# One TensorE loop for all eight V units of a decode attention kernel, and one PSUM bank for all rows of wo

## The chip, the cores and the metric

The kernel runs on one core of a Trainium2 chip. The metric is the device time of one execution in microseconds. The profile is one execution taken by the hardware profiler; its times count from the span's start. The engines are TensorE (PE; PEld is its loading of weights), VectorE (DVE), ScalarE (ACT), GpSimd (POOL) and SyncE (SP), which issues the loads. Each engine works its own list of instructions in order, and 16 DMA engines serve the transfers.

## The reference, cut to what matters

```
q = (x @ wq) as 32 heads of 128          # x: 2 x 1 x 512
scores = q k^T / sqrt(128)               # k_cache, v_cache: 2 x 32 x 4096 x 128, bf16
o = softmax(scores) @ v
a = o @ wo                               # wo: 4096 x 512
b = relu(x @ w1) @ w2                    # w1: 512 x 1376, w2: 1376 x 512
g = sigmoid(sum(x * gate_w))
return g * a + (1 - g) * b
```

K and V are 67 MB each; nearly all bytes are theirs.

## The kernel before, in words

The program is written as one list of instructions for each engine (`P.add` and its short forms `pe`, `dve`, `act`, `pool`, `sp`). The order of the calls from line 732 on is the order in each engine's list. `P.resolve` numbers the instructions that signal, and `P.emit` writes the lists with their waits. A `_Loop` in PE's list becomes a hardware loop (line 99), whose `head_slot` asks that its first instruction stand at the start of a block of instruction memory.

**Loads.** K and V are each eight units of 8 MB. SP issues all loads in one queue, in the order of `pieces` (line 247), into five SBUF regions of 4 MB (`kv`: A, Ah, B, Bh, C). A load waits until the region's last reader is done (`holder`, lines 253 to 264). V's units 0 to 6 are one load each, into A with Ah or B with Bh in turn; unit 7 is two loads, into B and Bh. Behind them stand w2x (the first 96 rows of w2), wo in two parts cut at row 24 of 32 (lines 340 to 342) and w2 in three parts into Ah (lines 343 to 345), which wait for V's unit 6 to be read.

**K.** DVE transposes each quarter of 1 MB (`k_turn`, 64 of them, line 477), PE multiplies it with q in a loop of eight turns run eight times (`k_scores`, lines 504 and 483). Line 483 is the helper `mm_held`, a matmul that uses the weights already loaded; groups of many places carry its number.

**Softmax and V's weights.** After `softmax` DVE spreads the transposed exponentials of a unit over eight columns (`v_spread`), so that they serve as matmul weights. Unit 0 has its weights in two halves (line 549).

**V.** Unit 0 (`v_unit`, line 588) uses weights of 32 columns: four matmuls at a time stand in the four column quarters of the array. Units 1 to 6 are a loop of two units run three times (`v_loop`, lines 617 and 483): weights of 64 columns, each used by two matmuls, into two PSUM banks. In the loop, counting semaphores stand for the usual waits: `sem_pt` (weights ready), `sem_v` (load landed) and `sem_rd` (the unit before is done). The two halves of unit 7 are `v_unit(7)` and `v_unit(8)`, 32 matmuls each. `v_extract` (lines 629, 641) takes a unit's result out of PSUM on DVE: for a loop unit three masked products, two of them on 32 partitions, then a sum.

**The end.** `o_gather(b)` adds up the units of one batch on PE (line 657), `o_scale(b)` scales the sum on DVE (line 663), `o_turn` turns it into `oW` (lines 669, 672). `project` (line 684) multiplies the four extra w2 rows (numbers -4 to -1) and wo's rows 0 to 23 into one PSUM bank in four column quarters; `pr_copy` (line 689) copies the bank to SBUF. `last_rows` multiplies wo's rows 24 to 31, then a row with `sel2` that adds up the copied bank, then w2's ten rows, all as small matmuls into the bank of the result (`fin_row`, line 697; `held_row`, lines 704 to 712). `store` copies the result out. `idle(n)` are n matmuls whose result nobody reads; they keep PE busy.

Of the kernel before, what the change touches and what calls it, by code (L numbers as in the profile page):

```python
# [17 lines left out]
WO_CUT = 24  # L18
WIDE = 5

# [37 lines left out]
class _Prog:  # L58
# [13 lines left out]
    def resolve(self):  # L72
        for e in self.ENGINES:
            n = 0
            for op in self.ops[e]:
                if isinstance(op, _Loop):
                    for m in range(op.n):
                        for step in op.ops:
                            if step.markers:
                                n += 1  # L80
                                step.markers[m].engine = e
                                step.markers[m].idx = n
                elif op.marker is not None:
                    assert op.marker.engine is None, "marker signalled twice"
                    n += 1
                    op.marker.engine = e
                    op.marker.idx = n

    def emit(self, engine, eng):
# [7 lines left out]
        for op in self.ops[engine]:  # L97
            if isinstance(op, _Loop):
                with self.nc.Fori(0, op.n, engines=(eng.engine,), head_slot={eng.engine: 0}):
                    for step in op.ops:  # L100
                        for sem, val in step.waits:
                            eng.wait_ge(sem, val)
                        ins = step.fn(eng)
                        if step.markers:
                            ins.then_inc(self.sems[engine], 1)
                continue
# [16 lines left out]
def bass_gated_mix__gqa_block_cached__dense_activation_relu__decode_kernel(  # L123
# [80 lines left out]
    V_BS = {0: 4, 7: 4, 8: 2}  # L204
    V_PAIRS = ((2, 3), (5, 6))
    V_LOOP = range(1, 7)
# [7 lines left out]
    O_C0 = MISC + 128  # L214
# [30 lines left out]
    v_pieces = [(u, both, "AB"[u % 2]) for u in range(7)] + [(7, lo, "B"), (7, hi, "Bh")]  # L245
# [9 lines left out]
    for kind, n, u, halves, region in pieces:  # L255
        parts = [region, region + "h"] if len(halves) == 2 else [region]
        predecessor[kind, n] = [m for r in parts for m in holder[r]]
        if kind == "v" and n in V_LOOP:
            landed[kind, n] = (sem_v[(n + 1) % 2], None)
# [227 lines left out]
    def k_scores():  # L487
# [27 lines left out]
        for bank in range(4):  # L515
            pe(lambda e, bank=bank: e.matmul(psf(0, 128, bank * BANK, 512), lhsT=ident16[:, :], rhs=zeros, start=False, stop=True),  # L516
               signal="pe_sc_end" if bank == 3 else None)

    def softmax():
# [10 lines left out]
        for g in range(2):  # L530
# [7 lines left out]
            v_spread_first(g)  # L538
        dve(lambda v: v.tensor_reduce(out=lrow[:], in_=lsum[:], axis=AX.X, op=ALU.add), waits=["act_exp3"], signal="dve_lrow")

    v_at = [0, 2, 4, 2, 4, 2, 4, 0, 1]

    def v_weights(n):
        nh = len(v_pieces[n][1])
        return ptm[:, 1024 * v_at[n]:1024 * (v_at[n] + nh)].rearrange("p (n h c) -> p n h c", h=8, c=4)

    def v_spread_first(g):
        rows, shape = slice(32 * g, 32 * g + 32), [128, 32, 8, 4]
        dve(lambda v: v.tensor_tensor(out=v_weights(0)[:, rows], in0=ET_sb[:, rows, 0:4].unsqueeze(2).to_broadcast(shape),  # L549
                                      in1=mask8[:].unsqueeze(1).unsqueeze(3).to_broadcast(shape), op=ALU.mult),  # L550
            waits=[f"dve_et{g}", "c_mask8"], signal=f"pt0{g}")

    def v_spread(n):
        u, halves, region = v_pieces[n]
        w0 = 4 * u + 2 * halves[0]
        waits = ["dve_et1", "c_mask8"] + ([f"v_read_{n - 2}"] if 3 <= n < 7 else ["v_read_0"] if n >= 7 else [])

        def spread(out, src, nc_, **kw):
            shape = [128, src.shape[1], 8, nc_]
            def fn(v):  # L560
                ins = v.tensor_tensor(out=out, in0=src.unsqueeze(2).to_broadcast(shape),  # L561
                                      in1=mask8[:].unsqueeze(1).unsqueeze(3).to_broadcast(shape), op=ALU.mult)
                return ins.then_inc(sem_pt[(n + 1) % 2], 1) if n in V_LOOP else ins
            dve(fn, waits=waits, **kw)

        if len(halves) == 2:
            spread(v_weights(n), ET_sb[:, :, w0:w0 + 4], 4)
        else:
            for r2 in range(2):
                spread(v_weights(n)[:, :, :, r2:4:2], ET_sb[:, 32 * r2:32 * r2 + 32, w0:w0 + 2], 2, signal=(f"pt{n}" if r2 else None))  # L570
# [4 lines left out]

    def v_unit(n):
        rows = v_moving(n)
        nn = rows.shape[2]
        for j in range(nn):
            t = j % 4  # L580
            waits = []
            if n == 0 and j % 32 == 0:
                waits = [f"pt0{j // 32}"]
            elif j == 0:
                waits = [f"pt{n}", "dve_m0" if n == 7 else "dve_m5"]

            def fn(e, j=j, t=t):
                ins = e.matmul(psf(32 * t, 32 * t + 32, V_BS[n] * BANK, 512), lhsT=v_weights(n)[:, j],  # L588
                               rhs=rows[:, :, j, :], start=(j < 4), stop=(j >= nn - 4), tile_position=(0, 32 * t))
                return ins.then_inc(sem_rd[1], 1) if n == 0 and j == nn - 2 else ins  # L590
            pe(fn, waits=waits, dwaits=([landed["v", n]] if j == 0 else []), signal=(f"v_read_{n}" if j == nn - 1 else None))

    def idle(n):
        out, lhsT, rhs = psf(0, 32, IDLE_C0, 512), ident16[:, 0:32], qbuf[:, :, :, :, 0:32]
        for j in range(n):
            if j:
                pe(lambda e: mm_held(e, out, lhsT, rhs, True, True, (128, 32), (0, 0)))
            else:
                pe(lambda e: e.matmul(out, lhsT=lhsT, rhs=rhs, start=True, stop=True, tile_position=(0, 0)), waits=["dve_m5"])

    def v_loop():
        loop = _Loop(len(V_LOOP) // 2)
        P.ops["pe"].append(loop)
        for x in range(2):
            n0 = V_LOOP[x]
            rows = v_moving(n0)
            for k in range(64):
                t, side = (k // 2) % 2, k % 2

                def fn(e, k=k, t=t, side=side, rows=rows, x=x, n0=n0):  # L610
                    out = psf(64 * t, 64 * t + 64, V_PAIRS[x][side] * BANK, 512)
                    lhsT = v_weights(n0)[:, k - side:k - side + 2].rearrange("p n h c -> p (n h c)")
                    start, stop = k < 4, k >= 60
                    if side:
                        ins = mm_held(e, out, lhsT, rows[:, :, k, :], start, stop, (128, 64), (0, 64 * t))
                    else:
                        ins = e.matmul(out, lhsT=lhsT, rhs=rows[:, :, k, :], start=start, stop=stop, tile_position=(0, 64 * t))  # L617
                    take = {0: (sem_pt[x], -1), 1: (sem_v[x], -16), 2: (sem_rd[1 - x], -1), 62: (sem_rd[x], 1)}.get(k)
                    return ins.then_inc(*take) if take else ins
                waits = [(sem_rd[1 - x], 1), (sem_pt[x], 1), (sem_v[x], 16)] if k == 0 else []  # L620
                marks = [marker(f"v_read_{V_LOOP[2 * m + x]}") for m in range(loop.n)] if k == 63 else None
                loop.ops.append(_Step(fn, waits, marks))

    def v_extract(n):
# [8 lines left out]
        waits = [f"v_read_{n}", "dve_maskc"] + ([f"dve_x{n - 1}"] if n else [])  # L633
        if n in V_LOOP:
            first, second = V_PAIRS[(n + 1) % 2]
            masked(first, 0, 128, waits, f"dve_ma{n}")
            masked(second, 32, 64, [f"dve_ma{n}"], f"dve_mb{n}")
            masked(second, 96, 128, [f"dve_mb{n}"], f"dve_m{n}")
        else:
            masked(V_BS[n], 0, 128, waits, f"dve_m{n}")  # L640
# [12 lines left out]
    def o_gather(b, part):  # L653
        mine = range(n_first) if b == 0 else range(n_first, len(v_pieces))
        for n in part:
            w0 = 24 - 8 * (v_pieces[n][0] - 4 * b)
            pe(lambda e, n=n, w0=w0: e.matmul(psf(0, 32, O_C0, 128), lhsT=selx[:, w0:w0 + 32], rhs=X2[:, b, n - mine[0], :],
                                              start=(n == mine[0]), stop=(n == mine[-1])),
               waits=[f"dve_x{n}"] + (["dve_rinv", "dve_selx"] + (["dve_O0"] if b else []) if n == mine[0] else []),
               signal=(f"pe_O{b}" if n == mine[-1] else None))  # L660

    def o_scale(b):
        dve(lambda v, b=b: v.tensor_scalar(out=O_sb[:, b, :], in0=psf(0, 32, O_C0, 128), scalar1=rinv[:, b:b + 1],
# [14 lines left out]
    def project(rows):  # L678
        for r in rows:
            t = r % 4  # L680
            lhsT, rhs = (hT[:, 14 + r, BOTH], w2x[:, t, :]) if r < 0 else (oW[:, r, BOTH], wreg[:, r * 512:(r + 1) * 512])
            dw = {-4: [(sem["w2x"], 32)], 0: [(sem["wo0"], 16)]}.get(r, [])
            waits = {-4: ["dve_h2", "dve_pr0"], 0: ["dve_oW"]}.get(r, [])
            pe(lambda e, t=t, r=r, lhsT=lhsT, rhs=rhs: e.matmul(psf(32 * t, 32 * t + 2, PR_C0, 512), lhsT=lhsT, rhs=rhs,
                                                               start=(r < 0), stop=(r >= WO_CUT - 4), tile_position=(0, 32 * t)),
               dwaits=dw, waits=waits, signal=("pe_pr" if r == WO_CUT - 1 else None))

# [28 lines left out]
    def last_rows():  # L716
        for r in range(WO_CUT, 32):
            fin_row(r == WO_CUT, False, oW[:, r, :], wreg[:, r * 512:(r + 1) * 512], [(sem["wo1"], 16)] if r == WO_CUT else [], [])
        fin_row(False, False, sel2[:, :], pr_sb, [], ["dve_pr", "dve_sel2"])
# [23 lines left out]
    v_spread(2)  # L743
    v_unit(0)
    o_denominators()
    v_loop()
    v_extract(0)
    for n in (last - 1, last):
        v_spread(n)
    for n in V_LOOP:  # L750
        v_extract(n)
        if n + 2 in V_LOOP:
            v_spread(n + 2)
    o_gather(0, range(n_first))
    o_scale(0)
    pr_clear()
    v_unit(last - 1)
    idle(6)
    v_extract(last - 1)
    o_gather(1, range(n_first, last - 1))  # L760
    idle(5)
    o_gather(1, (last - 1,))
    idle(13)
    v_unit(last)
    v_extract(last)
    project(range(-4, 0))
    idle(7)
# [4 lines left out]
    project(range(WO_CUT))  # L772
# [36 lines left out]
```

## Time and profile before

| | us |
|---|---|
| median of 3 runs (lowest, highest) | 343.67 (343.65, 343.81) |
| the profiled execution | 343.51 |
| its span, first to last instruction | 342.2 |
| busy: PE / DVE / ACT / POOL | 228.1 / 197.4 / 9.9 / 14.2 |
| mean granted TensorE clock | 0.865 |

A page of the profile has the busy time of each engine, the DMA queues, the chain of work that ended last, and the costliest groups by line. In the chain, each piece of work is followed back to what released it. In the timeline, "[1.25 <-DMA x]" means that the engine had sat idle for 1.25 us until the load of x landed. Ends of matmuls are modelled: the next may stream some 0.18 us before the end shown.

### The profile page before, as it was taken

The page shows a single profiled execution, that of the slowest core. Times are in us where ns is not written, and L with a number is a line of the kernel's source. Part 1 is how long each engine was busy: PE and PEld are TensorE (multiplying, and loading weights), DVE is VectorE, ACT ScalarE, POOL GpSimd, SP SyncE. Part 2 cuts the span into 40 slices and gives each one's busy share as a digit, 9 for nine tenths or more (in the row PEclk, how much of TensorE's full clock was granted, in tenths as well). Part 3 has the DMA queues.
Part 4 walks back from the last instruction along what each step waited for, and adds up shares of the span by engine and source line. Part 5 has one row for each costly group of instructions (what it writes and reads, how often), then busy time and mean ns, then how long its engine had stood idle before and what let it go on. Part 6 is the DMA issues. An engine that isn't in the chain of part 4 may idle for free.

```text
span 342.2 us, 2434 instructions
## 1 busy us (share of the span) xinstructions
PE 228.1 (67%) x1279; PEld 54.0 (16%) x770; DVE 197.4 (58%) x139; ACT 9.9 (3%) x29; POOL 14.2 (4%) x41
## 2 busy tenths in 40 slices
PE   0467329799969799689799463809172552909976
PEld 0111001111111111111111120202020110202313
DVE  1239059899889899698999496140606032020621
ACT  1051000000000000000000110000000000000000
POOL 6000000000000000000000200000000000000000
PEclk9999959989989899999999967856769585767999
DMA  8998989899999999898989999999989999989995
GB/s 349 429 490 370 483 375 483 371 486 414 444 467 391 426 433 483 383 475 375 483 383 475 398 467 423 429 467 391 483 383 475 391 467 391 467 387 433 426 421 241
DMA packets 3793, 145.50 MB, mean 425 GB/s; under 512 B 429, under 2 KB 564, under 8 KB 844
## 3 DMA queue, kind: packets, MB, share of 16 engines
q1 hardware_dynamic: 3782, 145.43, 98.6%
q8 instruction: 4, 0.07, 0.1%
q14 instruction: 1, 0.01, 0.0%
q10 hardware_dynamic: 6, 0.00, 0.0%
HBM read 145.43 MB, written 0.00 MB: 425 GB/s over the span
## 4 chain that ended last, share of the span: by engine, by line
DMA 63%; DVE 19%; PE 15%; issue 2%; ACT 0%; SPq 0%; DVEq 0%
DMA kv<-in_A_k_cache_dram 32%; DMA kv<-in_A_v_cache_dram 24%; DVE kt L477 17%; DMA kv<-in_B_w_dram 7%; PE PS L483 6%; PE PS L617 4%; PE PS L504 2%; PE PS L588 1%; DVE mpad L520 1%; ACT kt L532 0%; DVE kt L536 0%; DVE kt L549 0%; PE PS L697 0%; PE PS L516 0%; SPq L332 0%
## 5 line engine op out<-in xcount | busy, mean ns | idle before, releaser
L477 DVE STREAM_TRANSPOSE kt<-kv 128x2048 f32<-128x2048 f32 x64 | 141.2, 2274 | 25.7 <-DMA kv<-in_A_k_cache_dram 25.7
L504 PE MATMUL PS<-kt,qbuf 128*128 128x512 bf16 x256 | 106.2, 415 | 31.3 <-issue 23.0
L483 PE MATMUL PS<-kt,qbuf 128*128 128x512 bf16 x256 | 106.1, 415 | 0.0
L617 PE MATMUL PS<-kv,kt 128*64 128x512 bf16 x192 | 47.4, 471 | 55.2 <-DMA kv<-in_A_v_cache_dram 55.2
L629 DVE TENSOR_TENSOR kt<-PS,maskc 32x512 f32<-32x512 f32 (+1 forms) x21 | 14.5, 689 | 88.3 <-PE PS L483 81.3
L504 PEld LDWEIGHTS PS<-kt,qbuf 128*128 128x128 bf16 x256 | 25.7, 100 | 140.7 <-issue 140.7
L483 PE MATMUL PS<-kv,kt 128*64 128x512 bf16 x192 | 46.8, 465 | 0.0
L617 PEld LDWEIGHTS PS<-kv,kt 128*64 128x64 bf16 x192 | 15.2, 135 | 96.1 <-issue 96.1
L561 DVE TENSOR_TENSOR kt<-kt,mask 128x2048 bf16<-128x2048 bf16 (+1 forms) x10 | 16.2, 1656 | 0.0
L588 PE MATMUL PS<-kv,kt 128*32 128x512 bf16 x128 | 8.9, 432 | 8.6 <-DVE kt L549 7.3
L401 POOL TENSOR_TENSOR qbuf<-qs,mask 128x64 bf16<-128x64 bf16 x16 | 6.5, 406 | 160.7 <-PE PS L483 141.1
L641 DVE TENSOR_REDUCE kt<-kt 128x128 f32<-128x512 f32 x9 | 9.2, 1025 | 0.3
L483 PE MATMUL PS<-qbuf,ident 128*32 128x512 bf16 x37 | 9.0, 379 | 0.0
L406 PE MATMUL PS<-kv,xTw 128*32 128x320 bf16 (+1 forms) x32 | 5.3, 691 | 5.2 <-DMA kv<-in_A_wq_dram 3.2
L532 ACT ACTIVATE kt<-PS,negm 128x512 bf16<-128x512 f32 x4 | 2.7, 686 | 168.9 <-DVE negm L528 168.9
L588 PEld LDWEIGHTS PS<-kv,kt 128*32 128x32 bf16 x128 | 3.9, 107 | 15.6 <-DVE kt L549 7.8
L430 DVE CAST qrow<-PS 128x256 bf16<-128x256 f32 x2 | 2.6, 1524 | 5.7 <-PE PS L483 5.7
L729 ACT ACTIVATE out_sb<-PS 4x128 bf16<-4x128 f32 x1 | 0.3, 267 | 142.3 <-PE PS L712 142.3
L353 PE MATMUL PS<-ident,x_sb 3*128 3x3 bf16 x4 | 0.3, 166 | 6.2 <-DMA x_sb<-in_gate_w_dram 6.2
L520 DVE TENSOR_REDUCE mpad<-PS 128x2 f32<-128x2048 f32 x1 | 2.3, 2292 | 3.1 <-PE PS L516 3.1
L356 DVE COPY xT<-PS 128x12 bf16<-128x12 bf16 x1 | 0.2, 171 | 6.5 <-PE PS L353 6.5
L483 PE MATMUL PS<-kv,xTw 128*32 128x512 bf16 (+1 forms) x24 | 3.7, 511 | 0.0
(88 smaller groups left out, 53.6 us busy)
## 6 DMA issues: line engine op xcount, KB each, us to landing
kv<-in_A_k_cache_dram SPq DMA_DIRECT2D x4, 4096.0 KB, 29.4
kv<-in_A_v_cache_dram SPq DMA_DIRECT2D x2, 4096.0 KB, 23.5
kv<-in_A_wq_dram SPq DMA_DIRECT2D x1, 4096.0 KB, 14.8
kv<-in_A_wo_dram SPq DMA_DIRECT2D x1, 3072.0 KB, 33.4
kv<-in_B_w_dram SPq DMA_DIRECT2D x1, 1376.0 KB, 5.6
kv<-in_A_wo_dram SPq DMA_DIRECT2D x1, 1024.0 KB, 35.4
kv<-in_B_w_dram SPq DMA_DIRECT2D x1, 896.0 KB, 22.3
kv<-in_B_w_dram SPq DMA_DIRECT2D x1, 256.0 KB, 22.6
```

The lines of the kernel that those rows point to most:

```text
L401: pool(lambda g: g.tensor_tensor(out=out, in0=src, in1=mask, op=ALU.mult).then_inc(sem_q[k % 2], 1), waits=waits)
L406: return e.matmul(out, lhsT=xTw[:, t, :], rhs=rhs, start=(t == 0), stop=(t == 3), tile_position=(0, 32 * c))
L477: dve(lambda v: v.transpose(out=dst, in_=pairs[:, h, 64 * a:64 * a + 64, :]).then_inc(sem_kt[i % SPAN], 1), waits=([f"pe_sc_{i - NKT}"] if ...
L483: return e.add_instruction(mybir.InstMatmult(start_tensor_calc=start, stop_tensor_calc=stop, tile_size=size, tile_position=at, ldweights=F ...
L504: ins = e.matmul(out, lhsT=lhsT, rhs=rhs, start=False, stop=False)
L520: dve(lambda v: v.tensor_reduce(out=mpad[:, 0:2], in_=psf(0, 128, 0, 4 * BANK).rearrange("p (par n) -> p par n", par=2), axis=AX.X, op=ALU ...
L532: act(lambda a, g=g, par=par: a.activation(out=E_sb[:, 32 * g:32 * g + 32, 16 * par:16 * par + 16], in_=psf(0, 128, (2 * par + g) * BANK, ...
L561: ins = v.tensor_tensor(out=out, in0=src.unsqueeze(2).to_broadcast(shape), in1=mask8[:].unsqueeze(1).unsqueeze(3).to_broadcast(shape), op= ...
L588: ins = e.matmul(psf(32 * t, 32 * t + 32, V_BS[n] * BANK, 512), lhsT=v_weights(n)[:, j], rhs=rows[:, :, j, :], start=(j < 4), stop=(j >= n ...
L617: ins = e.matmul(out, lhsT=lhsT, rhs=rows[:, :, k, :], start=start, stop=stop, tile_position=(0, 64 * t))
L629: dve(lambda e: e.tensor_tensor(out=parts[p0:p1], in0=psf(p0, p1, bank * BANK, 512).rearrange("p (c d) -> p c d", c=4), in1=maskc[p0:p1].u ...
L641: dve(lambda e: e.tensor_reduce(out=X2[:, b, k, :], in_=parts.rearrange("p c d -> p d c"), axis=AX.X, op=ALU.add), waits=[f"dve_m{n}"], si ...
```

## The change

- V's unit 7 becomes one load (`v_pieces`), and all eight units are one PE loop of two units run four times, 64 matmuls of 32-column weights each, into bank 4 or 5. `v_unit`, the 64-column pairs and the second banks go. `sem_rd`, which tells the loop that the unit before is done, gets its first count from the first closing matmul of the scores.
- Behind the even unit of each round stand 55 idle matmuls: one, and an inner loop of nine run six times.
- Both loops are written without `head_slot`.
- Unit 0 waits for both halves of its weights, and stands behind the two denominator matmuls. `v_spread(2)` moves behind `v_extract(0)`.
- `v_extract` is one masked product and the sum for every unit.
- All earlier gathers on PE, and `o_scale(0)` on DVE, stand behind the loop and ahead of unit 7's extract; the second batch's gather has a bank of its own. `pr_clear` moves up. The idle matmuls there: `idle(6)`, `idle(5)` and `idle(13)` go, `idle(7)` becomes `idle(4)`.
- `project` takes all 32 rows of wo, waiting for wo's second part at row 24; `pr_copy` comes after all of them, and `last_rows` begins with sel2's row.

The diff, cut to its core:

```diff
-                with self.nc.Fori(0, op.n, engines=(eng.engine,), head_slot={eng.engine: 0}):
+        with self.nc.Fori(0, loop.n, engines=(eng.engine,)):
...
-    v_pieces = [(u, both, "AB"[u % 2]) for u in range(7)] + [(7, lo, "B"), (7, hi, "Bh")]
+    v_pieces = [(u, both, "AB"[u % 2]) for u in range(8)]
...
+            def close(e, bank=bank):
+                ins = e.matmul(psf(0, 128, bank * BANK, 512), lhsT=ident16[:, :], rhs=zeros, start=False, stop=True)
+                return ins if bank else ins.then_inc(sem_rd[1], 1)
...
     def v_loop():
-        loop = _Loop(len(V_LOOP) // 2)
+        loop = _Loop(len(v_pieces) // 2)
         P.ops["pe"].append(loop)
         for x in range(2):
-            n0 = V_LOOP[x]
-            rows = v_moving(n0)
-            for k in range(64):
-                t, side = (k // 2) % 2, k % 2
+            rows = v_moving(x)
+            for j in range(64):
+                t = j % 4
...
+                    ins = e.matmul(psf(32 * t, 32 * t + 32, V_BANK[x] * BANK, 512), lhsT=v_weights(x)[:, j], rhs=rows[:, :, j, :],
+                                   start=(j < 4), stop=(j >= 60), tile_position=(0, 32 * t))
...
+            if x == 0:
+                out, lhsT, rhs = psf(0, 32, IDLE_C0, 512), ident16[:, 0:32], qbuf[:, :, :, :, 0:32]
+                loop.ops.append(_Step(lambda e: e.matmul(out, lhsT=lhsT, rhs=rhs, start=True, stop=True, tile_position=(0, 0)), [], None))
+                inner = _Loop(IDLE_ROUNDS)
+                for j in range(IDLE_EACH):
+                    inner.ops.append(_Step(lambda e: mm_held(e, out, lhsT, rhs, True, True, (128, 32), (0, 0)), [], None))
+                loop.ops.append(inner)
...
-        if n in V_LOOP:
-            first, second = V_PAIRS[(n + 1) % 2]
-            masked(first, 0, 128, waits, f"dve_ma{n}")
-            masked(second, 32, 64, [f"dve_ma{n}"], f"dve_mb{n}")
-            masked(second, 96, 128, [f"dve_mb{n}"], f"dve_m{n}")
-        else:
-            masked(V_BS[n], 0, 128, waits, f"dve_m{n}")
+        masked(V_BANK[n % 2], 0, 128, [f"v_read_{n}", "dve_maskc"] + ([f"dve_x{n - 1}"] if n else []), f"dve_m{n}")
...
-                                                               start=(r < 0), stop=(r >= WO_CUT - 4), tile_position=(0, 32 * t)),
-               dwaits=dw, waits=waits, signal=("pe_pr" if r == WO_CUT - 1 else None))
+                                                               start=(r < 0), stop=(r >= WO_ALL - 4), tile_position=(0, 32 * t)),
+               dwaits=dw, waits=waits, signal=("pe_pr" if r == WO_ALL - 1 else None))
...
-        for r in range(WO_CUT, 32):
-            fin_row(r == WO_CUT, False, oW[:, r, :], wreg[:, r * 512:(r + 1) * 512], [(sem["wo1"], 16)] if r == WO_CUT else [], [])
-        fin_row(False, False, sel2[:, :], pr_sb, [], ["dve_pr", "dve_sel2"])
+        fin_row(True, False, sel2[:, :], pr_sb, [], ["dve_pr", "dve_sel2"])
...
     v_spread(1)
-    v_spread(2)
-    v_unit(0)
     o_denominators()
     v_loop()
-    v_extract(0)
-    for n in (last - 1, last):
-        v_spread(n)
-    for n in V_LOOP:
+    pr_clear()
+    for n in range(last):
         v_extract(n)
-        if n + 2 in V_LOOP:
+        if n + 2 <= last:
             v_spread(n + 2)
     o_gather(0, range(n_first))
+    o_gather(1, range(n_first, last))
     o_scale(0)
-    pr_clear()
-    v_unit(last - 1)
-    idle(6)
-    v_extract(last - 1)
-    o_gather(1, range(n_first, last - 1))
-    idle(5)
-    o_gather(1, (last - 1,))
-    idle(13)
-    v_unit(last)
     v_extract(last)
     project(range(-4, 0))
-    idle(7)
+    idle(4)
     o_gather(1, (last,))
     o_scale(1)
     o_turn()
     idle(8)
-    project(range(WO_CUT))
+    project(range(WO_ALL))
     idle(4)
     pr_copy()
     last_rows()
```

## The prediction

> **What bounds the kernel now.** I read the page's DMA queues first, then the chain of waits, then the timeline of the last 40 us, because the first two say that only the end can move.
>
> ```profile
> span 342.2 us, 2434 instructions
> q1 hardware_dynamic: 3782, 145.43, 98.6%
> q8 instruction: 4, 0.07, 0.1%
> ```
>
> The queue q1 carries all loads, and its packets fill 98.6% of 16 engines' span. The missing 1.4% is 4.8 us, about what lies before the first packet and after the last landing. So nothing that TensorE (PE) or VectorE (DVE) does in the middle can pay unless it starves the queue; the change moves the same 145 MB. The time is the landing of the last loads plus what is done after them. The chain of waits, in order of time, ends so (start, us, what):
>
> ```profile
> 278.88 29.07 DMA kv<-in_A_v_cache_dram
> 317.01 22.33 DMA kv<-in_B_w_dram
> 339.39 1.17 PE PS L697 x36
> 340.71 0.28 DVE out_sb L728
> ```
>
> It goes from V's unit 6 to w2's rows, landing at 339.38; PE multiplies them (L697, held row 340.39), DVE and ACT copy out (340.71), the store ends the span at 342.25. V's own tail is not in the chain: the timeline shows it beside the landing of wo (start, us, engine, line; in brackets the wait before it).
>
> ```profile
> 327.42 1.91 PE L588 MATMUL PS<-kv,kt 128*32 128x512 bf16 x32 [1.25 <-DMA kv<-in_A_v_cache_dram]
> 329.38 0.69 DVE L629 TENSOR_TENSOR kt<-PS,maskc 128x512 f32<-128x512 f32 x1 [6.47 <-PE PS L588]
> 330.11 1.04 DVE L641 TENSOR_REDUCE kt<-kt 128x128 f32<-128x512 f32 x1
> 331.19 0.41 PE L657 MATMUL PS<-kt,selx 128*32 128x128 f32 x2 [0.15 <-DVE kt L641]
> 332.31 0.39 PE L599 MATMUL PS<-qbuf,ident 128*32 128x512 bf16 x1
> 334.83 1.47 PE L684 MATMUL PS<-kv,oW 128*2 128x512 bf16 x24 [0.62 <-DMA kv<-in_A_wo_dram]
> 336.35 0.69 DVE L689 COPY kt<-PS 128x512 f32<-128x512 f32 x1 [3.59 <-PE PS L684]
> 337.21 0.87 PEld L697 LDWEIGHTS PS<-kv,oW 128*4 128x4 bf16 x32 [1.20 <-DMA kv<-in_A_wo_dram]
> 338.10 0.60 PE L697 MATMUL PS<-kt,sel 128*4 128x128 f32 x8
> 339.38 0.98 PEld L697 LDWEIGHTS PS<-kv,hT 128*4 128x4 bf16 x36 [0.97 <-DMA kv<-in_B_w_dram]
> ```
>
> Everything here waits for a load: project for wo's first part (334.83), the last eight rows for its second (337.21), w2's rows for theirs (339.38). The slack is small: the turn's copy into oW is over at 332.76, the idle matmuls at about 334.0, and sel2's row 0.7 us before w2 lands.
>
> **The middle, at nothing.** V's units 1 to 6 change from pairs of 64 columns (8.9 us a unit, 308.08 to 317.01, at a clock of 0.55 to 312.1 and then 1.00) to fours of 32 columns. Line 588 shows that shape: four matmuls share 0.43 us at half clock (200.03 to 200.46) and 0.2155 us at full, so a unit is 3.5 to 6.9 us. It frees its region sooner, but the next load then only queues longer. DVE loses two small masked products a unit and waits for loads anyway. The 55 idle matmuls behind each even unit take 55 x 0.2155 = 11.9 us on PE and delay unit 1 (211.30 in the trace) to about 220; its region is then free near 223.6, before V2 lands (230.53). All of that lies under q1.
>
> **The last unit, on the path.** Unit 7 was two loads, the first half multiplied from 317.70; now it is one, complete when the second half was, at about 327.4.
> - Start: unit 6 starts at 308.1 at half clock. 16 groups at 0.2155, made longer by half of the 2.7 to 6.5 us until the clock rises (2.8 us in unit 0, 6.1 in unit 2), end at 313 to 314.8; the idle matmuls end at 325 to 326.6. PE is free when V lands: no delay.
> - Matmuls: 64 are 16 x 0.2155 + 0.18 = 3.63 us against 1.91. Unit 7 ends at 331.05, +1.72.
> - A new wait. Both gathers of earlier units now stand behind the loop in PE's order, and DVE's order has o_scale(0), which waits for the first, ahead of unit 7's extract. The gather is 8 passes, 1.06 us (316.89 in the trace, 0.08 before the modelled end of the unit); the scale takes 0.40. So the extract starts at 331.05 - 0.08 + 1.06 + 0.04 + 0.40 + 0.03 = 332.50 instead of 0.05 after the unit's end: +1.40 more. PE's own queue behind the unit (gathers 0.81 and 0.64, four rows of w2x 0.22, idle(4) 0.86) ends before the extract does, so it hides.
> - Extract to gather: 0.73 + 1.04 + 0.04, at 334.31. From gather to the idle matmuls the trace has 1.12 us (331.19 to 332.31): 335.43. idle(8) is 8 x 0.2155 = 1.72, and project queues behind it: 337.15, where it waited for wo until 334.83. The slack of 2.0 us is gone and 2.3 us are lost.
>
> **wo through one bank.** Project now takes 32 rows: 8 x 0.2155 + 0.18 = 1.90 us, over at 339.05; row 24 is reached at 338.44, after its load (337.21). The 32 small matmuls of rows 24 to 31 (0.84 us) go. The copy of the bank, formerly early (336.35) and hidden under wo's second part, now comes after all rows: 0.05 + 0.69, at 339.79. Sel2's row starts at 339.84; 8 passes start 43 ns apart, so w2's rows start near 340.2 against 339.39. All of w2 has landed by then: 1.00 us to the held row as before, at 341.2 against 340.39. **Sum: +0.8 us.** Had the last unit not been late, the moved copy would end at 337.21 + 0.61 + 0.74 = 338.56 and sel2's row at 339.0, still hidden: it costs because the unit is late.
>
> The profiled execution took 343.51 (span 342.2 and 1.3 around it): 343.51 + 0.8 = 344.3. The median shown is 343.67, 0.16 above it, so I forecast 344.5. Unsure are the loop's exit (0.1), sel2's row (0.15) and when the one load lands (0.2 either way): 344.1 to 344.9 for this case.
>
> **Prices without a row.** The first unit now starts only after both halves of its weights and the denominators (202.6 instead of 199.62) and ends at 208.1 to 209.7, where it ended at 204.66. V2's load is issued then. From issue to landing the smallest transfer (the store, 341.02 to 342.2) takes 1.2 us, so data come at 209.4 to 211.0; unit 1 finds V1 landed at 211.30. Nothing is lost, by 0.2 to 1.8 us; lost would be at most about 1 us.
> The loops lose the alignment of their first instruction, and V's body grows from 192 to 256 matmuls and weight loads, with idle ones besides. The page shows four instruction packets: 0.1% of 16 x 342.2 us is 5.5 us, some 1.4 us each on one DMA engine. A load lands when its slowest engine is done, and in the windows 338 to 339 and 339 to 340 the DMA share falls to 0.61 and 0.24: some engines are about a microsecond behind the others. So one fetch more or fewer on the slowest engine moves landings by 1.4 us either way. I take nothing, the nearest case, since fetches have hit few engines so far.
>
> **Rivals.**
> - *Fewer fetches, faster or the same (0.10).* The PE program gets shorter. If the engine that sets V's last landing loses one fetch less, unit 7 starts 1.4 us sooner and all terms follow: 344.5 - 1.4 = 343.1. It decides from 0.8 us on. For it: the falling DMA share. Against: one early fetch is enough to make a straggler.
> - *The tail stays hidden, the same (0.12).* If the gather before o_scale(0) and sel2's row overlap better than the modelled ends say, 0.8 us vanish: 343.7.
> - *More fetches, slower (0.13).* [...] Over 16 fetches hit engines twice: landings 1.4 us later, 345.9. If the small idle loop itself fetched in each of its six rounds, unit 7 would start many microseconds late; I see no reason for that.
> [...]
> - *The clock falls, slower (0.10).* If PE has dropped to half clock when unit 7 starts, 3.4 us of it run at half speed: +1.7, 346.2. The gap between the idle matmuls and V's landing is 0.8 to 2.4 us. In the trace a stretch of 3.4 us with 1.42 us of busy PE (257.5 to 260.9) kept full clock, and one with 0.82 (278.0 to 281.4) lost it. Only the longest gap comes near.
> [...]
> - *V2 issued late, slower (0.05):* 345.5.
>
> **How the numbers follow.** The forecast has 0.50. A measurement of this kernel can tell 0.2%, 0.7 us, from no change; the line lies at 344.36, inside the forecast's own range, so a quarter of it (0.12) counts as same. Same: 0.12 + 0.12 + 0.04 of the first rival = 0.28. Faster: 0.06. Slower: 0.38 + 0.13 + 0.10 + 0.05 = 0.66. The range runs from 343.4 to 346.2, the hidden tail to the fallen clock, and leaves out some 0.15.
>
> **What would show it.** Unit 7: 64 matmuls in 3.6 us from about 327.4; o_scale(0) between its end and its extract; project not waiting for wo; w2's rows waiting for sel2's row and no longer for DMA; their start near 340.2. A chain that still ends with w2's landing refutes the sum; a landing of V other than 327.4 and a number on q8 other than 4 point to the fetches; unit 7 over 5 us long, to the clock.

## The result, and the profile after

| | us |
|---|---|
| before, median of 6 runs (lowest, highest) | 343.76 (343.65, 343.81) |
| after, median of 6 runs (lowest, highest) | 346.25 (345.21, 347.16) |
| ratio, 95% interval | 1.0074 (1.0056 to 1.0092) |
| the profiled execution of after, and its span | 347.16, 345.9 |

The kernel became slower, by 2.5 us at the median where 0.8 was forecast, and its runs now spread over 2 us where they spread over 0.2. The profiled execution is the slowest of the six, so its distances are the upper end of what the change does. It is 3.65 us longer than the profiled execution of before (347.16 against 343.51).

The page of after, span and DMA queues (packets, MB, share of 16 engines' span):

```profile
span 345.9 us, 2803 instructions
...
q1 hardware_dynamic: 3638, 145.43, 97.6%
q8 instruction: 3, 0.05, 0.1%
```

The same 145.43 MB take a smaller share of a longer span: 2.4% of 345.9 us is 8.3 us without loading, where it was 4.8. Of these 3.5 us more, 2.7 lie behind the last packet of w2 (it ends at 340.37 of 345.9, in before at 339.44 of 342.2); the rest must be looked for earlier. Instruction packets are one fewer, not more.

The timeline of the last 18 us (start, us, engine, line, tiles, count; in brackets the wait before it):

```profile
328.74 5.32 PE L582 MATMUL PS<-kv,kt 128*32 128x512 bf16 x64 [2.47 <-DMA kv<-in_A_v_cache_dram]
...
334.95 0.40 DVE L629 TENSOR_SCALAR O_sb<-PS,rinv,gb 32x128 bf16<-32x128 f32 x1 [18.70 <-PE PS L623]
...
335.28 0.67 DVE L602 TENSOR_TENSOR kt<-PS,maskc 128x512 f32<-128x512 f32 x1
...
339.70 2.10 PE L650 MATMUL PS<-kv,oW 128*2 128x512 bf16 x26
...
341.86 0.69 DVE L655 COPY kt<-PS 128x512 f32<-128x512 f32 x1 [3.25 <-PE PS L650]
342.61 0.61 PE L663 MATMUL PS<-kt,sel 128*4 128x128 f32 x8
...
343.05 1.17 PE L663 MATMUL PS<-kv,hT 128*4 128x128 bf16 x36
```

The order is the forecast's: unit 7 in one piece, o_scale(0) (L629) between it and its extract (L602), all of wo (L650) with no wait for a load, the copy behind it, sel2's row, and w2's rows (the last line), no longer waiting for DMA. But it starts later and takes longer: V's last load is found at 328.74 instead of 327.42 (+1.3), and its 64 matmuls take 5.32 us instead of 3.63 (+1.7). With the forecast's +0.8 for the rest that is 3.8, against 3.65 measured. So two things have to be explained.

The first is at the other end of V. Around V's unit 0, the timeline of after:

```profile
202.75 5.44 PE L582 MATMUL PS<-kv,kt 128*32 128x512 bf16 x64
...
208.27 0.33 SPq L341 DMA_DIRECT2D kv<-in_A_v_cache_dram  x1
...
231.96 4.46 PE L582 MATMUL PS<-kv,kt 128*32 128x512 bf16 x40 [8.45 <-DMA kv<-in_A_v_cache_dram]
```

and of before:

```profile
199.62 5.04 PE L588 MATMUL PS<-kv,kt 128*32 128x512 bf16 x64 [7.33 <-DVE kt L549]
...
204.74 0.33 SPq L335 DMA_DIRECT2D kv<-in_A_v_cache_dram  x1
...
230.66 0.64 PE L617 MATMUL PS<-kv,kt 128*64 128x512 bf16 x2 [9.89 <-DMA kv<-in_A_v_cache_dram]
```

Unit 0 starts 3.1 us later (202.75 against 199.62) and SP issues the load that takes its region, V2's, 3.5 us later. V2 is then found landed 1.3 us later (231.96 against 230.66): the same 1.3 us by which unit 7 is late. (The line at 231.96 is cut off at the end of its window; the unit has 64 matmuls.) The windows of 205 to 215 us (start:end, length, PE, PEld, DVE, ACT and POOL busy with counts, granted clock, DMA share, GB/s), before and then after:

```profile
205.00:215.00 10.00, 3.70 (x18) 1.00 (x10) 5.85 (x9) 0.00 (x0) 0.00 (x0) 0.72 0.98 421
```

```profile
205.00:215.00 10.00, 10.00 (x81) 1.23 (x41) 4.13 (x4) 0.00 (x0) 0.00 (x0) 0.93 0.89 360
```

The DMA share falls from 0.98 to 0.89, and the rate from 421 to 360 GB/s. The packets in the trace of after show why. Of the 16 DMA engines, 14 finish V1 between 208.97 and 209.44, the slowest only at 210.82. V2's first packet starts at 209.22, 0.95 us behind the issue, and those 14 engines get theirs between 209.22 and 210.43. An engine waits 0.43 us on average, and its first packet of V2 takes 0.53 us longer than the usual 2.42: about 1 us of each engine is lost. In before no engine waits there. A share over a short window can hide this, since it counts each packet whole where it starts (in after it is 1.48 for 209 to 211 us and 0.79 for 211 to 215).

The engine that ends V2 last (231.40; the next at 230.79) met something else besides: it carried an instruction packet at 222.74, in the middle of V2's load, for 0.96 us, and the data packet behind that took 2.89 us instead of 2.42. On another engine, one that hadn't waited, these 1.4 us could have stayed hidden. So, read this way, 0.6 us of the 1.3 come from the two meeting on one engine.

The second is the clock in unit 7, two windows of after:

```profile
326.20:329.70 3.50, 1.03 (x17) 0.58 (x20) 0.00 (x0) 0.00 (x0) 0.00 (x0) 0.95 0.98 421
329.70:333.10 3.40, 3.40 (x40) 1.59 (x36) 0.00 (x0) 0.00 (x0) 0.00 (x0) 0.55 1.02 441
```

In the first, PE is busy for 1.03 of 3.5 us, between the last idle matmuls and V's landing; in the second, it is fully busy and is granted 0.55.

### The profile page after: what moved, and what is told of

It reads as the page before. It is cut to its first block, busy times and chain, and to the rows that moved or that the text cites. A ratio compares the mean times of both kernels' runs of the same rounds, so it can differ in the third digit from the quotient of the medians.

```text
span 345.9 us, 2803 instructions
## 1 busy us (share of the span) xinstructions
PE 241.8 (70%) x1446; PEld 51.8 (15%) x937; DVE 186.8 (54%) x122; ACT 9.9 (3%) x29; POOL 14.2 (4%) x41
## 3 DMA queue, kind: packets, MB, share of 16 engines
q1 hardware_dynamic: 3638, 145.43, 97.6%
HBM read 145.43 MB, written 0.00 MB: 420 GB/s over the span
## 4 chain that ended last, share of the span: by engine, by line
DMA 60%; DVE 20%; PE 17%; issue 2%; ACT 0%; SPq 0%; DVEq 0%
DMA kv<-in_A_k_cache_dram 32%; DMA kv<-in_A_v_cache_dram 28%; DVE kt L483 17%; PE PS L582 6%; PE PS L489 6%; PE PS L510 2%; DVE kt L556 1%; DVE kt L544 1%; DVE mpad L528 1%; PE PS L650 1%; PE PS L663 0%; ACT kt L540 0%; PE PS L623 0%; DVE kt L607 0%; PE PS L523 0%
## 5 line engine op out<-in xcount | busy, mean ns | idle before, releaser
L582 PE MATMUL PS<-kv,kt 128*32 128x512 bf16 x512 | 39.5, 468 | 45.5 <-DMA kv<-in_A_v_cache_dram 45.5
L602 DVE TENSOR_TENSOR kt<-PS,maskc 128x512 f32<-128x512 f32 x8 | 5.5, 688 | 85.6 <-PE PS L582 85.6
L489 PE MATMUL PS<-qbuf,ident 128*32 128x512 bf16 x229 | 50.6, 379 | 0.0
L582 PEld LDWEIGHTS PS<-kv,kt 128*32 128x32 bf16 x512 | 17.1, 114 | 113.0 <-issue 106.0
L556 DVE TENSOR_TENSOR kt<-kt,mask 128x2048 bf16<-128x2048 bf16 (+1 forms) x9 | 18.4, 2046 | 0.1
L629 DVE TENSOR_SCALAR O_sb<-PS,rinv,gb 32x128 bf16<-32x128 f32 x2 | 0.8, 398 | 19.2 <-PE PS L623 19.2
L607 DVE TENSOR_REDUCE kt<-kt 128x128 f32<-128x512 f32 x8 | 8.2, 1025 | 0.3
L544 DVE STREAM_TRANSPOSE kt<-kt 128x1024 bf16<-128x1024 bf16 x2 | 2.5, 1240 | 1.5 <-ACT kt L540 1.5
```

What stands on the lines that cost most here:

```text
L489: return e.add_instruction(mybir.InstMatmult(start_tensor_calc=start, stop_tensor_calc=stop, tile_size=size, tile_position=at, ldweights=F ...
L544: dve(lambda v, g=g: v.transpose(out=kt_late[:, 2048 + 1024 * g:3072 + 1024 * g].rearrange("p (r w) -> p r w", w=32), in_=E_sb[:, 32 * g:3 ...
L556: ins = v.tensor_tensor(out=v_weights(n)[:, rows], in0=ET_sb[:, rows, 4 * n:4 * n + 4].unsqueeze(2).to_broadcast(shape), in1=mask8[:].unsq ...
L582: ins = e.matmul(psf(32 * t, 32 * t + 32, V_BANK[x] * BANK, 512), lhsT=v_weights(x)[:, j], rhs=rows[:, :, j, :], start=(j < 4), stop=(j >= ...
L602: dve(lambda e: e.tensor_tensor(out=parts[p0:p1], in0=psf(p0, p1, bank * BANK, 512).rearrange("p (c d) -> p c d", c=4), in1=maskc[p0:p1].u ...
L607: dve(lambda e: e.tensor_reduce(out=X2[:, b, k, :], in_=parts.rearrange("p c d -> p d c"), axis=AX.X, op=ALU.add), waits=[f"dve_m{n}"], si ...
```

## The experiments

Theory A: V2's load is issued so late that most DMA engines run out of work before its data come, and what is lost there is never made up; the forecast's tail is right. Its rivals: theory B, the fallen clock in unit 7 makes the difference; and theory C, the loops' new places in instruction memory do. Each kernel below is the changed one with the edit shown. `warm(n)`, which some of them add, are n idle matmuls of 32 columns into bank 6, which is free then. The kernel before, measured beside the runs x, y and z, took 343.75, 343.71 and 343.71 (medians of 19, 31 and 16 runs).

### x1: unit 0 at full clock

```
+    warm(42)
     o_denominators()
     v_loop()
```

> 42 idle matmuls on TensorE from the last closing matmul of the scores to the denominators, so that V's unit 0 meets a full clock; the rest is the changed kernel. Theory A (V2's load is issued too late: 208.27, and the DMA share falls to 0.8 in 209 to 211, so V's last landing is 1.2 us later): unit 0 takes 3.6 us instead of 5.44, V2 is issued near 206.4, no DMA gap, V7 lands near 327.4 instead of 328.5, about 345.0 against 346.25. Theory B (the surplus over the forecast is only the clock that fell in unit 7): landing of V7 unchanged in effect, 346.2. Theory C (instruction fetches delay the landings): they remain, V7 still lands past 328, 346.2.

Measured: 344.34 (344.13 to 344.45, 10 runs), ratio 1.0017 (1.0007 to 1.0027). The idle matmuls stand where PE waited for the softmax. They raise the clock before unit 0 (granted 1.00 from 196 to 200 us, where after has 0.53), so that it ends sooner. Timeline, then the window:

```profile
202.50 3.64 PE L590 MATMUL PS<-kv,kt 128*32 128x512 bf16 x64
...
206.21 0.33 SPq L341 DMA_DIRECT2D kv<-in_A_v_cache_dram  x1
...
230.72 5.46 PE L590 MATMUL PS<-kv,kt 128*32 128x512 bf16 x64 [9.27 <-DMA kv<-in_A_v_cache_dram]
...
327.48 3.72 PE L590 MATMUL PS<-kv,kt 128*32 128x512 bf16 x64 [1.50 <-DMA kv<-in_A_v_cache_dram]
...
332.01 0.40 DVE L637 TENSOR_SCALAR O_sb<-PS,rinv,gb 32x128 bf16<-32x128 f32 x1 [16.05 <-PE PS L631]
...
338.93 0.69 DVE L663 COPY kt<-PS 128x512 f32<-128x512 f32 x1 [3.25 <-PE PS L658]
339.67 0.61 PE L671 MATMUL PS<-kt,sel 128*4 128x128 f32 x8
340.11 1.17 PE L671 MATMUL PS<-kv,hT 128*4 128x128 bf16 x36
```

```profile
205.00:215.00 10.00, 10.00 (x66) 0.42 (x13) 4.07 (x4) 0.00 (x0) 0.00 (x0) 1.00 0.99 426
```

Unit 0 takes 3.64 us instead of 5.44, V2 is issued 2.06 us sooner, the DMA share is 0.99 again and by the packets the engines hardly wait (0.01 us on average); V2 is found at 230.72 and V7 at 327.48, as before the change. Of the 2.5 us of the change 1.9 are gone, and so is the spread. What is left, 0.6 us, is the tail, to which the forecast gave 0.8. The instruction packet is there too, at 216.51. Its engine again ends V2 last, at 230.16, but the next ends at 230.09: it had the time to spare. (The expectation's share of 0.8 isn't at 209 to 211 in the trace of after, where the windows show 1.48; 0.79 stands at 211 to 215.)

### x2: unit 0 later still

```
     o_denominators()
+    warm(10)
     v_loop()
```

> The opposite: 10 idle matmuls between the denominators and unit 0, so that unit 0 ends about 2.1 us later (half clock for the first of them). Theory A: V2 is issued near 210.4, all engines idle 2.1 us more, V7 lands near 330.6 and the time is 346.25 + 2.1 = 348.3. Theories B and C: a PE delay ahead of a loading-bound stretch costs nothing, 346.2.

Measured: 347.69 (347.27 to 348.18, 4 runs), ratio 1.0119 (1.0102 to 1.0136). Timeline and window:

```profile
210.66 0.33 SPq L341 DMA_DIRECT2D kv<-in_A_v_cache_dram  x1
...
330.45 3.64 PE L590 MATMUL PS<-kv,kt 128*32 128x512 bf16 x64 [1.39 <-DMA kv<-in_A_v_cache_dram]
```

```profile
205.00:215.00 10.00, 10.00 (x92) 1.87 (x62) 4.13 (x4) 0.00 (x0) 0.00 (x0) 0.90 0.75 301
```

Here the dose moves the other way, and the answer has the right sign and most of the size: V2 issued 2.39 us later than in after, unit 7 1.71 us later (2.1 were expected), DMA share down to 0.75. The engines wait 2.47 us on average for V2's data, which begin 0.96 us behind the issue and reach the last engine 1.92 us behind it. As in after, the engine with the instruction packet (224.45) ends V2 last, at 233.12, and the next at 232.08. Unit 7 ran at full clock in this trace, so the late load and the tail alone, without a clock fallen there, make this execution (347.31) 3.6 us slower than before.

### x3: unit 7 at full clock, V2 still late

```
-IDLE_ROUNDS, IDLE_EACH = 6, 9
+IDLE_ROUNDS, IDLE_EACH = 7, 9
```

> Seven rounds of nine idle matmuls behind each even unit instead of six: 1.94 us more, which closes the gap ahead of unit 7 (2.47 us in the trace of the changed kernel) to about 0.5. Theory B: full clock in unit 7 in every execution, 3.7 us instead of 5.32, and where the clock fell 1.7 us are gained: no run above 345.7, median about 345.3, smaller spread than 345.2 to 347.2. Theory A alone: V7 still lands near 328.5, no better than 345.2. If neither, unchanged 346.2.

Measured: 346.00 (345.28 to 347.09, 4 runs), ratio 1.0076 (1.0059 to 1.0093). Timeline:

```profile
207.97 0.33 SPq L341 DMA_DIRECT2D kv<-in_A_v_cache_dram  x1
...
328.19 3.64 PE L582 MATMUL PS<-kv,kt 128*32 128x512 bf16 x64 [0.69 <-DMA kv<-in_A_v_cache_dram]
```

Nine more idle matmuls in the round shorten the gap ahead of unit 7 from 2.47 to 0.69 us, and in the traced execution the clock holds. Median and spread stay where after has them, so theory B's forecast (no run above 345.7) fails. V2 is still late in its packets: they start 0.09 us late on average, and the first ones take 0.50 us longer, though the DMA share of 205 to 215 us is 0.99 here. The fallen clock is real where it comes, as in the profiled execution of after, but it isn't what moves the median. x4, with the edits of x1 and x3 together, asks the same from the other side.

> Both: unit 0 at full clock and seven idle rounds. A and B together: only the tail's forecast is left, 0.8 us over the kernel before: 344.5, with a spread below 0.5 us; V7 lands near 327.4, w2's rows wait for sel2's row at 340.2. If the tail's sum was wrong too, the distance from 344.5 tells by how much.

Measured: 344.46 (344.38 to 345.26, 10 runs), ratio 1.0023 (1.0014 to 1.0033): no better than x1 alone, and with a spread of 0.9 us where less than 0.5 was expected (two of the ten runs, 344.90 and 345.26, lie above the others).

### z2: the loops back at the start of a block

```
-        with self.nc.Fori(0, loop.n, engines=(eng.engine,)):
+        with self.nc.Fori(0, loop.n, engines=(eng.engine,), head_slot={eng.engine: 0} if outer else None):
```

> The changed kernel with both outer loops starting at the head of a block of instruction memory again, nothing else. Theory C (code fetched in the loops costs): 346.2 falls towards 344.3. Theory A (V2's load is late): no difference beyond the spread, 345.2 to 347.2, since the page already shows three instruction packets instead of four.

Measured: 346.39 (345.35 to 347.20, 4 runs), ratio 1.0083 (1.0067 to 1.0098). The time of after, and three instruction packets as in after. So theory C, the loops' new places, falls. What one instruction packet in V2's load costs, this run does not test: it has one there too, at 226.78.

### y1 to y4: the terms of the tail, with V2 on time

All four have x1's `warm(42)`. y1 takes away the wait that was worth +1.40 in the forecast:

```
-    o_scale(0)
     v_extract(last)
+    o_scale(0)
```

> All on the kernel of x1_warm_unit0 (344.34), where only the tail's 0.7 us are left. Here o_scale(0) stands behind unit 7's extract on VectorE instead of ahead of it. Theory (the tail's sum): the extract starts 0.05 us after the unit's end instead of 1.5, all terms move up by 1.4, w2's rows wait for their load again (339.4) and the time falls to the loads' end, 343.7. Rival (the gathers on TensorE hold up what follows anyway): less than 0.3 gained, 344.1 or more.

Measured: median 344.08 (343.55 to 345.52, 10 runs), ratio 1.0018 (1.0002 to 1.0033), in two groups: six runs from 343.55 to 344.33, and four from 345.33 to 345.52. The traced execution (345.45) is of the second:

```profile
327.52 5.41 PE L590 MATMUL PS<-kv,kt 128*32 128x512 bf16 x64 [2.31 <-DMA kv<-in_A_v_cache_dram]
...
332.96 0.69 DVE L610 TENSOR_TENSOR kt<-PS,maskc 128x512 f32<-128x512 f32 x1 [17.77 <-PE PS L590]
```

The extract now starts with the unit's end (327.52 + 5.41 = 332.93) where x1 had the scale's 0.40 us and the gather before it. The unit itself met the fallen clock (5.41 us, 3.72 in x1). The gap ahead of it is 2.31 us here and 2.47 in after, both with the clock fallen; it is 1.50 in x1 and 1.39 in x2, both with the clock kept. In x1 this extract starts 1.14 us behind the unit (331.20 to 332.34). The gap follows from unit 6, in which, by its time, the clock rose sooner or later (in after it was granted 0.50 up to 312.2 and 1.00 from 312.3 on, 2.9 us into the unit): unit 6 took 5.04 us in after, 5.20 here and 6.00 in x1, and with the gap behind the idle matmuls that makes 7.5 us each time.

y2 takes away six of the idle matmuls that project queues behind:

```
-    idle(8)
+    idle(2)
     project(range(WO_ALL))
```

> On x1_warm_unit0: two idle matmuls instead of eight ahead of project. Theory: project's first rows no longer queue behind them (in x1's trace oW is ready at 335.68, the idle ones stream to 336.97): 1.2 us sooner, 0.7 of it paid until the loads' end, 343.7. Rival (the idle matmuls stand in one column quarter and delay only a quarter of the rows): 0.3 at most, 344.0 or more.

Measured: 343.69 (343.32 to 344.82, 10 runs; seven below 343.9), ratio 1.0006 (0.9995 to 1.0018). Timeline:

```profile
335.89 2.14 PE L658 MATMUL PS<-kv,oW 128*2 128x512 bf16 x32
...
338.09 0.69 DVE L663 COPY kt<-PS 128x512 f32<-128x512 f32 x1 [2.25 <-PE PS L658]
...
339.61 1.17 PE L671 MATMUL PS<-kv,hT 128*4 128x128 bf16 x36 [0.17 <-DMA kv<-in_B_w_dram]
```

Project's 32 rows now run without a break, the copy is done at 338.78, and w2's rows wait for their load again, as before the change: the tail is hidden, and the kernel is level with before. The three runs above (344.64 to 344.82) have no trace.

y3 puts the cut of wo back (rows 24 to 31 as small matmuls, the copy ahead of them):

```
-WO_ALL = 32
+WO_ALL = 24
...
+        for r in range(WO_CUT, 32):
+            fin_row(r == WO_CUT, False, oW[:, r, :], wreg[:, r * 512:(r + 1) * 512], [(sem["wo1"], 16)] if r == WO_CUT else [], [])
+        fin_row(False, False, sel2[:, :], pr_sb, [], ["dve_pr", "dve_sel2"])
```

> On x1_warm_unit0: project takes wo's rows 0 to 23 again and rows 24 to 31 go as small matmuls beside the copy of the bank, as in the kernel before. Theory: 2 groups of 0.2155 and the copy (0.74) on the path are replaced by 0.86 of small rows that hide the copy: 0.3 gained, 344.0. Rival (the moved copy alone costs its whole 0.74, or all rows in one bank cost nothing): 343.6, or 344.3.

Measured: 344.76 (344.50 to 346.77, 10 runs), ratio 1.0044 (1.0027 to 1.0062). The expectation failed: seven runs lie at 344.5 to 344.8, above x1 and not below it, and three, without a trace, at 346.4 to 346.8. Timeline:

```profile
338.00 0.22 PE L671 MATMUL PS<-kv,oW 128*4 128x128 bf16 x1
338.21 0.38 PE L571 MATMUL PS<-qbuf,ident 128*32 128x512 bf16 x1
...
338.44 0.69 DVE L663 COPY kt<-PS 128x512 f32<-128x512 f32 x1 [2.81 <-PE PS L658]
...
338.87 1.21 PE L671 MATMUL PS<-kv,oW 128*4 128x128 bf16 x29
...
339.97 0.60 PE L671 MATMUL PS<-kt,sel 128*4 128x128 f32 x7
340.30 1.22 PE L671 MATMUL PS<-kv,hT 128*4 128x128 bf16 x35
```

The copy is indeed early (over at 339.13, in x1 at 339.62). But PE's list has the idle matmuls first, and nearly all small rows (x29) come only behind them, from 338.87: sel2's row follows them at 339.97, not the copy at 339.13. With the idle matmuls where they are, the one bank is the cheaper of the two ways once the unit is late.

y4 has all three edits.

> On x1_warm_unit0: the three edits together. Theory: the tail has 2 us of slack and the time is that of the loads' end, as in the kernel before: 343.5 to 343.8, no gain over y1 or y2. If the fewer instruction packets (3 instead of 4) were worth something, it would be below 343.3.

Measured: 344.43 (343.60 to 344.77, 10 runs), ratio 1.0016 (1.0006 to 1.0025). The expectation failed again: two of ten runs (343.60 and 343.66) are where all ten were expected, and a third is near (343.90). In the traced one (344.33) unit 7 took 5.41 us behind a gap of 2.31: the fallen clock again. Whether all the others fell for the same reason isn't known, since they have no trace.

### z1 and z3: the cures together, and without the first

z1 has x1's `warm(42)`, x3's seven rounds and the edits of y1 and y2.

> Full clock in unit 0 (x1), seven idle rounds, o_scale(0) behind the last extract (y1) and idle(2) ahead of project (y2); wo stays in one bank. If the loss was V2's late load, the tail behind the last unit, and in some executions a fallen clock, nothing of it is left: 343.5 to 343.8 in every execution, level with the kernel before (ratio 1.000), and w2's rows wait for their load near 339.4. If the fall of the clock comes from something other than the gap ahead of unit 7, executions near 345.4 remain, as in y1.

Measured: 343.83 (343.48 to 344.67, 11 runs), ratio 1.0001 (0.9992 to 1.0010): level with before, with a spread of 1.2 us. The traced execution is its slowest (344.67):

```profile
340.55 1.17 PE L671 MATMUL PS<-kv,hT 128*4 128x128 bf16 x36 [0.17 <-DMA kv<-in_B_w_dram]
```

w2's own load is late here, by 1.2 us against before (339.39), and so are all loads from V2 on (V2 is found at 231.90, in x1 at 230.72), although V2 was issued at 206.38. The packets name the engine: the one that ends V2 last (231.33; the next at 230.28) took 3.79 us for its first packet of V2 instead of 2.42, and then carried the instruction packet (at 217.82, 0.96 us, with 2.89 us for the data packet behind it). Why that first packet was slow stays open (below).

z3 has seven rounds and the edits of y1 and y2, but leaves unit 0 as in after (5.44 us there, granted 0.50 until 206.4).

> The changed kernel with the tail's cures alone (seven rounds, o_scale(0) moved, idle(2)), unit 0 left at half clock. Theory A: the loads' end itself is late by what V2 lost, so slack in the tail buys back at most the 0.7 us of the tail and the clock: 344.8 to 345.8 with a spread of a microsecond or more. If the tail was the cause of the whole 2.5 us, 343.7.

Measured: 345.15 (344.27 to 345.70, 5 runs), ratio 1.0042 (1.0028 to 1.0055).

```profile
208.15 0.33 SPq L341 DMA_DIRECT2D kv<-in_A_v_cache_dram  x1
...
340.05 1.17 PE L663 MATMUL PS<-kv,hT 128*4 128x128 bf16 x36 [0.18 <-DMA kv<-in_B_w_dram]
```

With the whole tail hidden, w2's rows wait for their load, 0.7 us later than before even in this execution, the fastest of the five. V2's first packets started 0.21 us late on average and took 0.46 us longer. The median is 1.4 us above before and 1.3 above z1. That is theory A by itself: the loads end late where V2 is issued late.

No version beats the kernel before: y2 and z1 are level with it.

## Why the prediction was wrong

**What failed.** The step is, in "Prices without a row": "Nothing is lost, by 0.2 to 1.8 us". Its first half was right: V2 was issued at 208.27, inside the 208.1 to 209.7 that it gives. Two things were wrong in the second half.

The price of issue to data came from the smallest transfer, 1.2 us; in x2, where 14 of the 16 engines had run out, the engines got their first packet 0.96 to 1.92 us behind the issue, and these packets took 0.55 us longer than usual. And the time at which V2's data were needed was taken to be 211.30, when unit 1 finds V1 landed. That is the time of the slowest of 16 engines: by the packets in the trace of after, 14 of them had finished V1 by 209.44, and only two worked on, until 210.02 and 210.82. The two together can be sized by the runs. V2 issued 4.9 us ahead of 211.30 (206.39, y2) delayed unit 7 by 0.2 us at most (327.64 against x1's 327.48); issued 3.3 us ahead (207.97, x3) it delayed it by 0.71. In after, z3 and x2 the delay was 1.26, 0.67 and 2.97. An estimate that takes a microsecond of late issue to cost one puts the latest harmless issue at 208.27 - 1.26 = 207.0, 207.97 - 0.71 = 207.3, 208.15 - 0.67 = 207.5 and 210.66 - 2.97 = 207.7, so 3.6 to 4.3 us ahead of 211.30, where the forecast allowed 1.2. The forecast's "lost would be at most about 1 us" was too small for the same reason. The rival *V2 issued late* carried 0.05 and a price of +1.0; it was the case that came true, with 1.9 (after against x1, medians).

A second term was put at nothing in the same section: one fetch on the slowest engine, rightly priced at 1.4 us. The traces bear the price out (0.96 us for the packet and 0.47 more for the one behind it), and in after the fetch fell on the engine that ended V2 last. It cost 0.6 us there, 1.0 in x2, 0.3 and 0.2 in x3 and z3 and under 0.1 in x1, by the distance to the engine that ended V2 next. No run varies the fetch alone, so this share of the loss is read from traces and not shown by an experiment.

**The tail: right.** x1 has everything else as forecast and measures it alone: unit 7 at 327.48 (forecast 327.4) for 3.72 us (3.63), extract at 332.34 (332.50), project's rows behind the idle matmuls at 336.76 (337.15), copy over at 339.62 (339.79), sel2's row at 339.67 (339.84), w2's rows at 340.11 (340.2). Its profiled execution took 344.33, and the sum was 344.3. The new wait and the queue of idle(8) are both on the path: with either taken away at least half of the runs come to 343.3 to 343.8 (five of ten in y1, seven in y2), and in y2's trace w2's load is the bound again. The wait itself is 1.14 us in x1 against 1.45 (+1.40, and 0.05 that was there). What y3 expected, that the cut of wo put back would gain 0.3 us, didn't hold.

**The clock: right mechanism, chance too low.** "Only the longest gap comes near" is what happened: gaps of 2.31 and 2.47 us ahead of unit 7 lost the clock in the traces of y1, y4 and after, gaps of 1.39, 1.50 and 1.74 (x2, x1, y2) kept it, and the price was 1.7 us (5.32 or 5.41 against 3.64; in after the clock was granted 0.50 from 329.35 to 332.70 and 1.00 before and after it, so the forecast's 3.4 us at half speed are in the trace). The odd units inside the loop say the same: gaps of 2.29, 2.49 and 2.54 (y2, x2, y3) lost it, gaps of 2.05 and 2.11 (x1, z2) kept it. The forecast gave 0.10. In y1 four of ten runs lie 1.7 us above the fastest five, and the one of the four with a trace had lost it. In after, a stretch of 3.5 us with 1.03 us of busy PE (29%) was followed by half clock. It lies between the prediction's two rows of before, of which 1.42 us of 3.4 kept the clock and 0.82 lost it, so those rows left the longest gap open.

**More fetches: refuted.** The new loop body, 256 matmuls and weight loads with 11 idle ones, run four times, left three instruction packets on q8, where before had four; in the trace of after none falls between 223.70, in the first round, and 343.78, behind the loop. That a loop fetches in each of its rounds, which the rival's 345.9 and its 0.13 suppose, was the author's assumption and is shown by no run; no run here has a longer body of that loop.

**The middle: right**, from unit 2 on: with V2 on time, V7 lands at 327.48 against 327.42, with the whole loop rewritten.

**Open.** z1 keeps a spread of 1.2 us that before doesn't have. In its traced execution a slow first packet of V2 (3.79 us) and the instruction packet met on one DMA engine; what made the first packet slow, with V2 issued 0.17 us later than in x1, isn't known, and whether z1's other runs have the same cause isn't either. Why the engines lie apart by 1.9 us at V1's end (208.97 to 210.82) wasn't tested. A version in which V2 goes into a region that is free earlier, which would take unit 0 off the path, wasn't tried.

## What to carry to other kernels

Where a queue of loads is the bound, ask of every load when its region comes free, and compare that with when the *first* engines finish the load before it, not with when a reader finds that load landed; here the estimate is 3.6 to 4.3 us of lead. A first unit that runs at half clock because PE waited before it (here 9.81 us, and 5.44 us for the unit instead of 3.64) can be the one that starves the queue; idle matmuls in that wait paid back 1.9 of 2.5 us. And look at the spread as well as at the median: it was 2 us with V2 late and 0.3 in x1. But y1 and z1 spread with V2 early, so a wide spread names no cause.

## What the runs showed of the hardware that was not expected

- The queue lost time before the last packet of the load ahead was done. In after, V2 was issued 2.6 us before the slowest DMA engine ended V1 (208.27 to 210.82), and the engines still lost about 1 us each (0.43 of waiting, 0.53 of slower first packets). In x1, with 4.5 us (206.21 to 210.75), they lost 0.02.
- An instruction packet held up one DMA engine by 1.4 us: 0.96 for itself, and 2.89 instead of 2.42 us for the data packet behind it (after, x2, x3, z1). It showed in the landing where that engine had no time to spare.
- A stretch of 3.5 us with 1.03 us of matmuls in it was followed by half clock (after). Of the gaps ahead of V units in these traces, those of up to 2.11 us kept the clock and those from 2.29 us on lost it.
- Idle matmuls in one column quarter let only a few later matmuls pass. The idle ones stand in one quarter, and project's rows go to the four quarters in turn. In after, two groups of three rows run in between the idle matmuls, and the other 26, though most use other quarters, only behind them, at 339.70; with fewer idle matmuls, in y2, all 32 run in one piece.
- The PE loop over V, with 256 matmuls and weight loads and 11 idle ones in its body, caused no instruction packets in its later rounds (after: three on q8 in all, at 116.08, 222.74 and 343.78).
